# Putting all tiled matmuls of a chunk behind the first product's last rows, and eight banks as four and four

## The chip, the cores and the metric

The kernel runs on one core of a Trainium2 chip. The metric is the device time of one execution in microseconds (us). Engines are called by the profile's short names: PE (TensorE matmul), PEld (its weight load), DVE (VectorE), ACT (ScalarE), POOL (GpSimd) and SP (SyncE, which issues nearly all DMAs here, in order).

## The reference

An mLSTM cell over 4 batches x 8 heads x 768 steps of dimension 40, then a feed-forward layer with a squared ReLU over the 3072 resulting tokens:

```python
def _attn_ref(q, k, v, i_gate, f_gate, o_gate):
    for t in range(S):
        m_new = np.maximum(f_gate[:, :, t] + m, i_gate[:, :, t])
        f_stab = np.exp(f_gate[:, :, t] + m - m_new)
        i_stab = np.exp(i_gate[:, :, t] - m_new)
        m = m_new
        C = f_stab[..., None, None] * C + i_stab[..., None, None] * np.einsum('bhd,bhe->bhde', vt, kt)
        n = f_stab[:, :, None] * n + i_stab[:, :, None] * kt
        h_tilde = np.einsum('bhde,bhe->bhd', C, qt)
        nq = np.einsum('bhd,bhd->bh', n, qt)[:, :, None]
        y[:, :, t] = sigmoid(o_gate[:, :, t]) * h_tilde / np.maximum(np.abs(nq), 1.0)

def _moe_ref(x, w_in, w_out):          # x: 3072 x 320, w_in: 320 x 2048, w_out: 2048 x 320
    h = np.maximum(x @ w_in, 0.0)
    return h * h @ w_out
```

The weights w_in and w_out come as 64-bit floats.

## The kernel before

**Tiling.** The sequence is cut into 24 chunks of 128 steps (6 per batch). A chunk is worked in the parallel form: scores of keys against queries, times a matrix of decays W, give P; P times the values, plus the state C times the decayed queries, gives numerators and the denominator; the chunk's keys and weighted values, plus the decayed C, give the new C. Two chunks (256 tokens) make a token group of the feed-forward layer; there are 12 groups.

**Two stages.** The first stage (to about 100 us) handles chunks 0 to 5 with full-width matmuls while the 64-bit weights are rounded piece by piece (`Rounding`: `words` on ACT, `join` on DVE and POOL, one `step` is both). The second stage is one loop over `parts`, a list of triples (which product, group g, step i). Part n belongs to chunk s = 6 + n // 4 at place at = n % 4, so a chunk has four parts and a pair of chunks has eight: two steps of the second product of group g, four batches of the first product of group g+2, two more steps of the second product of group g. The steps of all engines are issued by hand in this loop's order (`manual_schedule`), and every engine and SP's queue work in that order.

**The first product** of a batch is `ffn1_main` (L634: full 128 x 128 tiles) and, for two batches together, `ffn1_rest` (L645: the last 64 of 320 rows, as two row tiles). ReLU on ACT (`relu_half`, L660) and squares on DVE (`square_half`, L667) follow. **The second product** is `ffn2` for group 0 (L674) and `ffn2_fast` after that (L728): seven products of half the width from sums of blocks, with DVE sums before (`sums`, L723) and after them (L744); the results leave by L764 and L769.

**A chunk of the second stage**, by functions: `load_squares` (L308) brings keys and queries in 32 x 32 squares and `turn_kq` (L315) turns them; `load_A` (L333), `decays` (L368), `mask` (L358), `weigh` (L382) make W; `scale_q` (L481) decays the queries; `scores` (L420, row tiles of 40 rows) and `weighted` (L433) make P. `attend_turned` puts the numerators (`numT`, L508 from C with 40 x 64 tiles, L517 from P with 128 x 64 tiles) into two PSUM banks, and the new C's product (`dC`, L527, 128 x 40 tiles) into a third; DVE turns numT (L534) and adds dC to the decayed C (L540; `decay_C`, L486).

**The relay.** A chunk's numerators then go to DRAM (`store_num`, L546) and back in another order (`load_num`, L551), `normalise_turned` (L563 to L572) divides, the rows go to DRAM (`store_rows`, L598) and back in squares (`load_rows`, L603), and `turn_squares` (L610) gives xT, which the first product of the chunk's token group reads. `pair_up` (L286) rearranges keys and queries of the chunk three later in DRAM. All these DMAs are in SP's queue, and each waits there for its data and for one of eight places.

**Places before.** At at = 0 `score` (scores and P); at at = 1, ahead of the part's product, `attend_turned`, then `decays`, `mask`, `turn_kq`, `decay_C`, `turn_squares` of the chunk before, `store_num`, `load`, `load_num`, `pair_up`; at at = 2 `scale_q`, and behind the product `weigh`, `normalise_turned`, `store_rows`, `load_squares`, `load_rows`, `load_A`; at at = 3 every fourth chunk the sigmoids. In a pair, the first chunk's tiled matmuls so stand between steps of the second product, and the second chunk's between batches of the first. The first product of group g+2 needs xT of the two chunks of the pair before.

**PSUM** has eight banks: attention 3 (`ps_at`), first stage's `ps_h` 3 and `ps_o` 2; in the second stage `ps_h` has 5.

Of the kernel before, what the change touches and what calls it, by code (L numbers as in the profile page):

```python
# [9 lines left out]
F32 = mybir.dt.float32  # L10
# [7 lines left out]
P = 128  # L18
# [11 lines left out]
def kernel(  # L30
# [48 lines left out]
    prep = ctx.enter_context(tc.tile_pool(name="prep", bufs=2))  # L79
    work = ctx.enter_context(tc.tile_pool(name="work", bufs=2))  # L80
    xts = ctx.enter_context(tc.tile_pool(name="xts", bufs=2))
    ps_at = ctx.enter_context(tc.tile_pool(name="ps_at", bufs=3, space=PSUM))
    banks = ExitStack()
    ps_h = banks.enter_context(tc.tile_pool(name="ps_h", bufs=3, space=PSUM))
    ps_o = banks.enter_context(tc.tile_pool(name="ps_o", bufs=2, space=PSUM))
    ctx.enter_context(tc.manual_schedule())
# [29 lines left out]
    def make_consts():  # L116
        for t in kq_b:
            nc.vector.memset(t[:, :, :, D:], 0.0)
        for t in va_b:
            nc.vector.memset(t[:, :, D:], 1.0)  # L120
        for t in va_w:
            nc.gpsimd.memset(t[:, H * D1 :], 0.0)
        nc.vector.memset(keep[:], 1.0)
        nc.vector.memset(keep[:, :, 0:1], 0.0)
        make_identity(nc, ident[:])

        nc.gpsimd.memset(sel[:], 0.0)
        nc.gpsimd.affine_select(
            sel[:], sel[:], compare_op=ALU.not_equal, fill=1.0, base=0, pattern=[[-1, H], [0, P]], channel_multiplier=1,
        )  # L130

        nc.gpsimd.memset(later[:], 0.0)
        nc.gpsimd.affine_select(
            later[:], later[:], compare_op=ALU.is_ge, fill=-1e30, base=0, pattern=[[1, P]], channel_multiplier=-1,
        )

        nc.gpsimd.memset(bdm[:], 1.0)
        nc.gpsimd.memset(bdm[:DP, :, 1, :], 0.0)
        nc.gpsimd.memset(bdm[DP:, :, 0, :], 0.0)


    def in_words(ap):
# [20 lines left out]
    class Rounding:  # L163
# [56 lines left out]
        def done(self):  # L220
            return len(self.b)

        def step(self):
            if len(self.b) < len(pieces):
                if len(self.a) == len(self.b):
                    self.words()
                self.words()
                self.join()

    rounding = Rounding()  # L230
# [94 lines left out]
    def sigmoid(s):  # L325
        nc.scalar.activation(st[s]["og"], st[s]["og"], AF.Sigmoid)
# [71 lines left out]
    def bank(o=False):  # L398
        t = ps_o.tile([P, W], F32, name="tp", tag="o_ps") if o else ps_at.tile([P, W], F32, name="tp", tag="at")
        return t[:].rearrange("p (j t) -> p j t", j=PR)  # L400

    def transposes(s, o=(False, False)):
        d = st[s]
        kqT(s)
        for i, n in enumerate(("kT", "qT")):
            tp = bank(o[i])
            for j in range(PR):
                nc.tensor.transpose(  # L408
                    tp[:, j, :], d["kq"][:, i, 2 * j : 2 * j + 2, :].rearrange("p h d -> p (h d)"), ident[:],
                )  # L410
            (nc.scalar.copy if i == 0 or s in (0, *range(2, 7)) else nc.vector.tensor_copy)(d[n], tp)
# [79 lines left out]
    def attend_turned(s):  # L491

        b, c = divmod(s, NB)
        d = st[s]
        halves = [slice(DP * i, DP * (i + 1)) for i in range(2)]
        live = [slice(DP * i, DP * i + D) for i in range(2)]  # L500
        numT = [ps_at.tile([P, W], F32, name="numT", tag="at")[:].rearrange("p (c t) -> p c t", t=P) for _ in range(2)]

        if c > 0:
            C = C_b[(s - 1) % 2]
            for e in range(2):
                for i, g in ((0, 0), (1, 1), (0, 1), (1, 0)):
                    j = 2 * e + g
                    nc.tensor.matmul(  # L508
                        numT[i][halves[g], e, :], lhsT=C[live[i], j * D1 : j * D1 + DP], rhs=d["eA"][live[i], j, :],
                        start=(e == 0), stop=False, skip_group_check=True,  # L510
                    )
        for i in range(2):
            for e in range(2):
                for g in range(2):
                    j = 2 * e + g
                    h = PR * i + j
                    nc.tensor.matmul(  # L517
                        numT[i][halves[g], e, :], lhsT=va_w[s % NKQ][:, h * D1 : h * D1 + DP],
                        rhs=d["P"][h % 2][:, h // 2, :] if s < KQ_SQ else d["P"][i][:, j, :],
                        start=(c == 0 and e == 0), stop=True, skip_group_check=True,  # L520
                    )
        if c + 1 < NB:
            dC = ps_at.tile([P, PR, D1], F32, name="dC", tag="at")
            for j in range(PR):
                for i in range(2):
                    h = PR * i + j
                    nc.tensor.matmul(  # L527
                        dC[live[i], j, :], lhsT=d["kq"][:, 0, h, :D], rhs=d["vw"][:, h, :], start=True, stop=True,
                    )

        tn = attn.tile([P, P // SQ, PR, SQ], F32, name="tn", bufs=1)
        to = tn[:].rearrange("p m c r -> p c m r")
        for i in range(2):
            nc.vector.transpose(to[:, 2 * i : 2 * i + 2], numT[i][:, :2, :].rearrange("p c t -> p (c t)"))  # L534
        d["tn"] = tn
        if c + 1 < NB:
            Cn = C_b[s % 2][:, : PR * D1].rearrange("p (j d) -> p j d", d=D1)
            for rows in live:
                if c > 0:
                    nc.vector.tensor_tensor(Cn[rows], dC[rows], d["Cd"][rows], op=ALU.add)  # L540
                else:
                    nc.vector.tensor_copy(Cn[rows], dC[rows])
# [229 lines left out]
    def do(f, s):  # L772
        if 0 <= s < NT:
            f(s)
# [36 lines left out]
    load_part(1, 2)  # L811
    fetch(1)
    idle(12)
    transposes(0)
    idle(4)
    scores(0)
    idle(3)
# [45 lines left out]
    for u in range(8):  # L863
        s = 2 + u // 2
        relu_half()
        if u % 2 == 0:
            if u == 0:
                ffn1(0, 0)
                scores(s)
                rounding.step()  # L870
            else:
                turn_rows(s - 1)
                scores(s)
                ffn1(u // 4, u % 4)
            if u == 2:
                rounding.words()
            weighted(s)
            if u == 2:
                mask(s + 1)
                rounding.join()  # L880
# [6 lines left out]
        else:  # L887
# [6 lines left out]
            attend(s)  # L894
            if u == 3:
                square_half()
            rounding.join()
            normalise(s)
            for r in {5: (8,), 7: (9,)}.get(u, ()):
                load(r)  # L900
            for r in {5: (7,), 7: (8,)}.get(u, ()):
# [18 lines left out]


    banks.close()
    ps_h = ctx.enter_context(tc.tile_pool(name="ps_h", bufs=5, space=PSUM))
    before.close()
    attn = ctx.enter_context(tc.tile_pool(name="attn", bufs=1))
    C_b = [attn.tile([P, PR * D1 + 24], F32, name=f"C{i}") for i in range(2)]
# [7 lines left out]
        parts += [(2, g, i) for i in range(2, 4)]  # L934
    LAST = (21, 23, 25, 25, 26)
    assert LAST[-1] == len(pieces)
    for n, (which, g, i) in enumerate(parts):
        s, at = 6 + n // 4, n % 4
        if n == 5:
            brought.close()  # L940
            late = ctx.enter_context(tc.tile_pool(name="late", bufs=1, side="right"))
        if at == 0:
            do(score, s)
        if at == 1:
            do(attend_turned, s)
            do(decays, s + 1)
            do(mask, s + 1)
            if n > 4:
                do(turn_kq, s + 1)
            do(decay_C, s + 1)  # L950
            if s > X_SQ:
                do(turn_squares, s - 1)
            do(store_num, s)
            do(load, s + 4)
            if 8 <= s < 20:
                load_o(s + 4)
            do(load_num, s)
            do(pair_up, s + 3)
        if 5 <= n < 8:
            sums_of_weights(n - 5)  # L960
        if n == 6:
# [7 lines left out]
            sums(g + 1, slice(0, NPAIR), (2,))  # L969
        if which == 2 and g > 1 and i < 2:  # L970
            sums(g, slice(0, NPAIR), (3 + i,))
        if at == 2:
            if n > 4:
                do(scale_q, s + 1)
        if at == 3:
            if s % 4 == 3:
                for r in range(s + 1, min(s + 5, NT)):
                    sigmoid(r)
        if which == 1:
            ffn1_main(g, i)  # L980
            if i % 2 == 0:
                held = st["half"]
            else:

                both = held, st["half"]
                for more, half in enumerate(both):
                    ffn1_rest(g, i - 1 + more, half[0])
                for half in both:
                    st["half"] = half
                    relu_half()  # L990
                    square_half()
        elif g == 0:
            ffn2(g, *divmod(i, 2))
        else:
            ffn2_fast(g, i)
        if at == 2:
            do(lambda s: weigh(s, masked=True), s + 1)
            if n < 4:
                do(turn_kq, s + 1)
                do(scale_q, s + 1)  # L1000
            do(normalise_turned, s)
            do(store_rows, s)
            do(load_squares, s + 2)
            do(load_rows, s)
            do(load_A, s + 2)
        if n < 5:
            while rounding.done < LAST[n]:
                rounding.step()


# [28 lines left out]
```

## Time and profile before

| | us |
|---|---|
| median of 3 runs (lowest, highest) | 527.99 (525.57, 529.61) |
| the profiled execution's own time | 527.05 |
| its span | 525.2 |
| L634 on PE, 768 matmuls | 175.7 |
| L728 on PE, 528 + 352 + 176 + 176 matmuls | 77.0 + 52.3 + 25.7 + 25.7 |
| tiled matmuls L645, L420, L517, L508, L527 on PE | 49.0, 26.9, 19.7, 10.4, 7.2 |
| DMA issue to landing, median: A_bc, num_rows, numerators back, x_rows, xT | 4.7, 3.1, 2.2, 2.1, 2.3 |

The profile is of one execution. Times are from the start of the span. A line of a timeline has the start, the time until the merged instructions' end, engine, line, operation, what is written and read, and how many instructions were merged; "idle" in brackets is the engine's idle time before them and what ended it. Matmuls overlap, so their cost in place is best read as the difference of starts. A line of the list of waits has who waited for whom, the total, how often, and the longest. A float32 matmul appears as two records.

### The profile page before, as it was taken

How to read it: one execution, taken by the hardware profiler on the slowest of the kernel's cores; microseconds unless marked ns; L12 is line 12 of the kernel's file. 1: busy time of each engine (PE TensorE's matmuls, PEld its weight loads, DVE VectorE, ACT ScalarE, POOL GpSimd, SP SyncE). 2: the span in 40 equal slices, each digit the busy share in tenths (PEclk: the TensorE clock that was granted, in tenths of full speed). 3: DMA queues.
4: the chain of work that ended last, by engine and by line, in shares of the span. 5: the costliest groups of instructions: out<-in, count | busy, mean ns of one | idle time of the engine just before them, and what ended most of it. 6: DMA issues, size and time to landing. Idle time of an engine off the chain costs nothing.

```text
span 525.2 us, 10338 instructions
## 1 busy us (share of the span) xinstructions
PE 515.1 (98%) x3929; PEld 449.8 (86%) x3929; DVE 331.8 (63%) x638; ACT 194.2 (37%) x460; POOL 88.2 (17%) x110
## 2 busy tenths in 40 slices
PE   9989989998999999999999999999999999999997
PEld 4868878885798898898898898898898898998997
DVE  8588988968864764655754755665755755522541
ACT  3767577552541431522432623322623413102000
POOL 3355633231210210110210200110201210000000
PEclk9997999999999999999999999999999999999999
DMA  9989699777586586586586576676556262110000
GB/s 193 225 207 194 158 161 202 190 184 155 117 162 121 126 173 126 124 168 127 135 162 132 122 151 125 149 158 135 133 122 128 69 130 43 61 36 2 26 25 26
DMA packets 239394, 68.06 MB, mean 130 GB/s; under 512 B 185744, under 2 KB 233872, under 8 KB 239344
## 3 DMA queue, kind: packets, MB, share of 16 engines
q1 hardware_dynamic: 239248, 67.20, 60.5%
q8 instruction: 31, 0.51, 0.4%
q10 hardware_dynamic: 96, 0.20, 0.1%
q14 instruction: 19, 0.16, 0.1%
HBM read 55.08 MB, written 17.86 MB: 139 GB/s over the span
## 4 chain that ended last, share of the span: by engine, by line
PE 87%; DVE 5%; ACT 3%; DMA 2%; SPq 2%; issue 1%; POOL 0%; ACTq 0%; DVEq 0%; POOLq 0%
PE h_ps L728 33%; PE h_ps L634 27%; PE h_ps L645 7%; PE tp L420 4%; PE numT L517 3%; PE h_ps L674 2%; PE hp L456 2%; PE numT L508 2%; PE idle L787 1%; DVE g L667 1%; PE tp L408 1%; SPq L308 1%; DMA num_rows<-tn 1%; PE A_ps L349 1%; PE dC L527 1%
## 5 line engine op out<-in xcount | busy, mean ns | idle before, releaser
L634 PE MATMUL h_ps<-xT,w_in 128*128 128x256 f32 x768 | 175.7, 384 | 0.6 <-ACT xT L619 0.6
L634 PEld LDWEIGHTS h_ps<-xT,w_in 128*128 128x128 f32 x768 | 144.2, 191 | 22.0 <-issue 1.2
L667 DVE TENSOR_TENSOR g<-r_sb 128x512 f32<-128x512 f32 x96 | 61.7, 702 | 66.5 <-ACT r_sb L660 66.5
L660 ACT ACTIVATE r_sb<-h_ps 128x512 f32<-128x512 f32 x96 | 49.9, 600 | 108.6 <-PE h_ps L645 105.5
L728 PE MATMUL h_ps<-w_out,g 128*128 128x160 f32 x528 | 77.0, 302 | 0.0
L728 PEld LDWEIGHTS h_ps<-w_out,g 128*128 128x128 f32 x528 | 72.5, 190 | 1.4
L358 POOL TENSOR_SCALAR_AFFINE_SELECT A_bc<-A_bc 128x1024 f32<-128x1024 f32 x22 | 24.3, 1103 | 214.2 <-ACT kq L368 155.4
L382 ACT ACTIVATE W_sb<-A_bc,b_T 128x128 f32<-128x128 f32 x176 | 53.8, 390 | 13.3 <-POOL A_bc L358 13.1
L728 PE MATMUL h_ps<-T,S 128*128 128x160 f32 x352 | 52.3, 302 | 0.0
L728 PEld LDWEIGHTS h_ps<-T,S 128*128 128x128 f32 x352 | 48.8, 190 | 3.0 <-ACT r_sb L660 3.0
L368 ACT ACTIVATE kq<-A_bc 64x512 f32<-64x512 f32 x30 | 18.9, 629 | 84.3 <-DMA A_bc<-a_rows 84.2
L645 PE MATMUL h_ps<-xT,w_in 64*128 64x256 f32 x384 | 49.0, 391 | 0.0
L645 PEld LDWEIGHTS h_ps<-xT,w_in 64*128 64x128 f32 x384 | 34.8, 186 | 12.3 <-issue 9.0
L744 DVE TENSOR_TENSOR y_sb<-y_sb,h_ps 128x160 f32<-128x160 f32 x44 | 14.1, 320 | 29.3 <-PE h_ps L728 28.7
L433 DVE TENSOR_TENSOR P_sb<-tp,W_sb 128x512 f32<-128x512 f32 x46 | 29.5, 684 | 3.6 <-PE tp L420 3.1
L534 DVE STREAM_TRANSPOSE tn<-numT 128x256 f32<-128x256 f32 x36 | 15.7, 447 | 23.2 <-PE numT L517 23.2
L394 POOL TENSOR_TENSOR vw<-va,W_sb 128x328 f32<-128x328 f32 x20 | 18.1, 904 | 66.0 <-ACT W_sb L382 60.3
L748 ACT COPY y_sb<-h_ps 128x160 f32<-128x160 f32 x11 | 3.2, 293 | 66.3 <-PE h_ps L728 66.3
L420 PEld LDWEIGHTS tp<-kqT 40*128 40x128 f32 x384 | 24.2, 187 | 3.3 <-issue 2.3
L420 PE MATMUL tp<-kqT 40*128 40x128 f32 x384 | 26.9, 279 | 0.0
L728 PE MATMUL h_ps<-T,g 128*128 128x160 f32 x176 | 25.7, 299 | 0.0
L728 PE MATMUL h_ps<-w_out,S 128*128 128x160 f32 x176 | 25.7, 299 | 0.0
(119 smaller groups left out, 592.0 us busy)
## 6 DMA issues: line engine op xcount, KB each, us to landing
A_bc<-a_rows SPq DMA_DIRECT2D x23, 512.0 KB, 4.7
raw<-in_moe_w_out_dram SPq DMA_DIRECT2D x16, 320.0 KB, 3.5
num_rows<-tn SPq DMA_DIRECT2D x18, 256.0 KB, 3.1
kq<-num_rows SPq DMA_DIRECT2D x72, 64.0 KB, 2.2
kqT<-kq_rows SPq DMA_DIRECT2D x34, 128.0 KB, 3.2
raw<-in_moe_w_in_dram SPq DMA_DIRECT2D x8, 512.0 KB, 5.2
kq<-in_k_dram SPq DMA_DIRECT2D x24, 160.0 KB, 4.7
va<-in_v_dram SPq DMA_DIRECT2D x24, 160.0 KB, 4.9
```

The lines of the kernel that those rows point to most:

```text
L358: nc.gpsimd.affine_select(A[:], A[:], compare_op=ALU.is_ge, fill=-1e30, base=0, pattern=[[0, H], [1, P]], channel_multiplier=-1,)
L368: nc.scalar.activation(e[rows], st[s]["A"][0][rows, PR * i : PR * (i + 1), :], AF.Exp)
L382: nc.scalar.activation(d["W"][:, i * n + h, :], A[i][:, h, :], AF.Exp, bias=b_T[:, b, c, i * n + h : i * n + h + 1],)
L394: nc.gpsimd.tensor_tensor(d["vw"][:], d["va"][:], d["W"][:, :, P - 1 : P].to_broadcast([P, H, D1]), op=ALU.mult,)
L420: nc.tensor.matmul(sc[i][:, j, :], lhsT=d["kT"][rows, j, :], rhs=d["qT"][rows, j, :], start=True, stop=True,)
L433: nc.vector.tensor_tensor(t, d["sc"][i], d["W"][:, heads, :], op=ALU.mult)
L517: nc.tensor.matmul(numT[i][halves[g], e, :], lhsT=va_w[s % NKQ][:, h * D1 : h * D1 + DP], rhs=d["P"][h % 2][:, h // 2, :] if s < KQ_SQ els ...
L634: nc.tensor.matmul(hs[i][:, n, :], lhsT=w_in[:, a, fb * P : (fb + 1) * P], rhs=xT[:, :, a, :], start=(n == 0 and a == 0), stop=False,)
L645: nc.tensor.matmul(hs[i][:, n, :], lhsT=w_in2[rows, 2 * pp + n, :], rhs=xT[rows, :, 2, :], start=False, stop=(n == 1),)
L660: nc.scalar.activation(rs[-1][:], h[:], AF.Relu)
L667: nc.vector.tensor_tensor(g4[:, :, i, :], r[:], r[:], op=ALU.mult)
L728: nc.tensor.matmul(to, lhsT=lhsT[:, p], rhs=rhs[:, p, :], start=(start and p == 0), stop=(p == NPAIR - 1), skip_group_check=True,)
```

## The change

Arithmetic and numbers of matmuls, of DMAs and of DVE work stay. The diff, cut to its core:

```diff
-    def transposes(s, o=(False, False)):
+    def transposes(s, o=(False, False), apart=0):
         for i, n in enumerate(("kT", "qT")):
+            if i > 0 and apart:
+                idle(apart)
...
         numT = [ps_at.tile(...) for _ in range(2)]
+        dC = numT[1][:, 2:, :]...                  
+        def new_kv():
...
+                        dC[live[i], j, :], lhsT=d["kq"][:, 0, h, :D], rhs=d["vw"][:, h, :],
+                        start=False, stop=True, skip_group_check=True,
...
         if c > 0:
...
+            if c + 1 < NB:
+                new_kv()
         for i in range(2):
...
-        if c + 1 < NB:
-            dC = ps_at.tile([P, PR, D1], F32, name="dC", tag="at")
...
+        if c == 0:
+            new_kv()
...
-    transposes(0)
+    transposes(0, apart=4)
...
             if u == 0:
                 ffn1(0, 0)
                 scores(s)
+                weighted(s)
+                relu_half()
                 rounding.step()
...
             if u == 3:
                 square_half()
-            rounding.join()
-            normalise(s)
+                normalise(s)
+                rounding.join()
+            else:
+                rounding.join()
+                normalise(s)
...
-    ps_h = ctx.enter_context(tc.tile_pool(name="ps_h", bufs=5, space=PSUM))
+    ps_at = ctx.enter_context(tc.tile_pool(name="ps_at", bufs=4, space=PSUM))
+    ps_h = ctx.enter_context(tc.tile_pool(name="ps_h", bufs=4, space=PSUM))
...
+    def attended(s):
+        do(store_num, s)
+        do(load, s + 4)
+        if 8 <= s < 20:
+            load_o(s + 4)
+        do(load_num, s)
+        do(pair_up, s + 3)
+    def normalised(s, *between):
+        do(normalise_turned, s)
+        do(store_rows, s)
+        for f, r in between:
+            do(f, r)
+        do(load_rows, s)
+    def ffn1_batch(g, i, squares=True, tiled=lambda: None):
+        both = st["held"], st["half"]
+        for more, half in enumerate(both):
+            ffn1_rest(g, i - 1 + more, half[0])
+        tiled()
+        for half in both:
+            st["half"] = half
+            relu_half()
+        if squares:
+            square_half()
+            square_half()
...
+        r, a = (n % 8, 6 + 2 * (n // 8)) if n >= 8 else (None, None)
+        if n in (0, 4, 8):
             do(score, s)
+            if n == 4:
+                square_half()
+                square_half()
+        if n in (2, 5):
+            attend_turned(s)
...
+        if r == 0:
+            do(load_squares, a + 2)
+            do(load_A, a + 2)
+        elif r == 1:
+            do(turn_squares, a - 1)
+            do(decays, a + 1)
+            do(mask, a + 1)
+            do(turn_kq, a + 1)
+        elif r == 4:
+            do(scale_q, a + 1)
+            do(turn_kq, a + 2)
+        elif r == 5:
+            normalised(a)
+        elif r == 7:
+            normalised(a + 1)
         if which == 1:
             ffn1_main(g, i)
...
+                    x = a + i // 2
+                    def tiled():
+                        do(attend_turned, x)
+                        do(score, x + 1)
+                    ffn1_batch(g, i, tiled=tiled)
+                    do(decay_C, x + 1)
+                    attended(x)
...
+        if r == 2:
+            do(lambda s: weigh(s, masked=True), a + 1)
+        elif r == 3:
+            do(decays, a + 2)
+            do(mask, a + 2)
+        elif r == 4:
+            do(lambda s: weigh(s, masked=True), a + 2)
+            do(load_A, a + 3)
+        elif r == 5:
+            do(load_squares, a + 3)
+        elif r == 6:
+            do(turn_squares, a)
+            do(scale_q, a + 2)
+        elif r == 7 and (a + 1) % 4 == 3:
+            for t in range(a + 2, min(a + 6, NT)):
+                sigmoid(t)
```

What it does, in words. From part 8 on, a pair of chunks a, a+1 is ordered by r = n % 8. In the parts r = 3 and r = 5, behind `ffn1_rest`, PE now has in a row: the last rows of the first product, `attend_turned` of a chunk, and the scores of the next. Chunk a stands behind the first two batches, chunk a+1 behind the second two. The new C's product moves into the unused half of the second numerator bank and, but for a batch's first chunk, ahead of L517. The attention has four banks and the feed-forward four; the attention's pool of the first stage ends with that stage.

On SP, the order of a pair becomes: kqT squares and A_bc of a+2; for a: numerators out, loads of a+4, numerators back, `pair_up`; A_bc of a+3; x_rows and xT of a; for a+1: numerators out, loads, numerators back, `pair_up`; kqT squares of a+3; an output; x_rows and xT of a+1; an output. On DVE, normalise of a stands at r = 5 ahead of that part's work, normalise of a+1 at r = 7, the turn of xT of a at r = 6 and of a+1 at r = 1 of the next pair.

In parts 0 to 7, `attend_turned` of chunk 6 moves from part 1 to part 2 and the squares of part 3 move behind P of chunk 7 in part 4; the rounding steps there no longer work one piece ahead at the end. In the first stage, four filler matmuls stand between the transposes of the first keys and queries, P of chunk 2 and a ReLU move ahead of a rounding step, and `normalise` of chunk 3 moves ahead of a `join`. Four memsets on POOL move to the end of the constants.

## The prediction

> **What bounds the kernel now.** I read the page first (busy shares, then the chain that ended last), then TensorE's list of waits, then the timeline of one steady stretch engine by engine, and last the windows around the two longest waits, for the granted clock.
>
> ```profile
> span 525.2 us, 10338 instructions
> PE 515.1 (98%) x3929; PEld 449.8 (86%) x3929; DVE 331.8 (63%) x638; ACT 194.2 (37%) x460; POOL 88.2 (17%) x110
> PE 87%; DVE 5%; ACT 3%; DMA 2%; SPq 2%; issue 1%; POOL 0%; ACTq 0%; DVEq 0%; POOLq 0%
> ```
>
> TensorE is busy for 98% of the span and holds 87% of the chain. Its waits are few, and all of them lie before 128 us:
>
> ```profile
> PE numT L508 <- DVE P_sb L433: 2.6, 1, 2.6
> PE tp L618 <- DVE x_sb L587: 1.7, 1, 1.7
> PE dC L449 <- DVE P_sb L433: 1.1, 1, 1.1
> ```
>
> From 155 to 465 us TensorE waits for nobody. One pair of chunks there takes 39.71 us (first product of one token group at 273.00, of the next at 312.71). TensorE's timeline of the same pair shows what a change of tile shape costs:
>
> ```profile
> 286.47 0.67 PE L508 MATMUL numT<-kq,C 40*64 40x128 f32 x16
> 288.40 3.72 PE L634 MATMUL h_ps<-xT,w_in 128*128 128x256 f32 x16
> 293.98 2.44 PE L728 MATMUL h_ps<-T,S 128*128 128x160 f32 x16
> 296.25 2.34 PE L728 MATMUL h_ps<-T,g 128*128 128x160 f32 x16
> 298.43 2.34 PE L728 MATMUL h_ps<-w_out,S 128*128 128x160 f32 x16
> 300.69 1.16 PE L420 MATMUL tp<-kqT 40*128 40x128 f32 x16
> ```
>
> Starts are to be subtracted: a product of L728 takes 2.18 us between like products (296.25 to 298.43) and about 2.27 beside a tiled one.
>
> The second thing to see is a relay off the critical path: what `attend_turned` computes goes to DRAM, back, through `normalise_turned`, to DRAM and back again before the first product (L634) of its token group may start. For chunk 17:
>
> ```profile
> 328.40 0.34 SPq L546 DMA_DIRECT2D num_rows<-tn  x1
> 331.45 1.85 SPq L551 DMA_DIRECT2D kq<-num_rows  x4
> 338.27 0.17 DVE L563 TENSOR_SCALAR dm<-kq 128x8 f32<-128x8 f32 x1
> 340.09 0.38 SPq L598 DMA_DIRECT2D x_rows<-x_sb  x1
> 343.35 2.16 SPq L603 DMA_DIRECT2D xT<-x_rows  x4
> 349.07 0.54 DVE L610 STREAM_TRANSPOSE xT<-xT 128x384 f32<-128x384 f32 x1
> 351.52 1.67 PE L634 MATMUL h_ps<-xT,w_in 128*128 128x256 f32 x7
> ```
>
> Its tiled matmuls began at 326.18, the user at 351.52: 25.3 us, with 1.9 to spare at the end.
>
> **The tile switches, pair by pair.** Nothing is computed less: the same matmuls run in another order. Before, one pair has five tiled groups on TensorE; after, two, each L645, L508, L527, L517, L420 in a row. Products: 6.71 + 4.54 + 4.45 = 15.70 before; all seven stand together after, 2.27 + 6 x 2.18 = 15.35. First product: 7.00 + 3.65 + 3.65 = 14.30 before, two runs of 7.00 after. Tiled matmuls: 9.7 before (1.83 + 1.93 for L645, 0.99 + 1.09 for L420, twice 0.60 + 0.92 + 0.41); after, between 4.85 and 5.05 a group, since L517 now meets another shape (1.02 as at 326.78) and L420 costs 0.99 or 1.09: 9.7 to 10.1. Sum 39.05 to 39.45, so 0.26 to 0.66 gained; I take 0.5, over eight pairs **-4.0 us**.
>
> **The banks.** The second product's pool goes from 5 banks to 4, the attention's from 3 to 4. With 4 each batch of the first product finds its banks freed by the ReLUs (2.06 us for four) about 2 us before it needs them, because the tiled group (2.95 us) stands between. The sum onto y (L744) that the third product of a half must wait for comes after transposes, new C, P and squares on VectorE (0.89 + 0.62 + 1.28 + 2.50 from the numerators' end at 1.9 us into the group), at 7.3 to 7.6 us, and that product may start at 7.4: 0.0 to 0.3 us a pair, hidden behind the wait told next.
>
> **The relay.** This is the term that decides. Let 0 be the start of a pair's first product. The second chunk's tiled group started at 13.5 us before; after, it stands behind both runs and both L645 groups: 7.00 + 1.93 + 2.95 + 7.00 + 1.90 = 20.8. The next pair's first product is due at 39.2, so the relay has 18.4 us instead of 25.3. Its steps, with the trace's durations and the new order of the queues:
> - numerators turned: L517 starts 1.0 us into the group (L508 and L527 first) and the second transpose ends 1.59 after that (326.78 to 328.37): 23.4.
> - The store of this chunk now stands in SP's queue behind the first chunk's x_rows and xT. That one's tn ends at 11.5; from there to numerators back in SBUF the trace shows 6.7 to 8.2 us where no A_bc load goes just ahead (odd chunks): 18.4; normalise 1.8: 20.3; x_rows 2.1 to land, four xT loads 2.1 to issue: **24.7**, 1.3 after tn is ready. A new A_bc load is issued shortly before that x_rows; numerator stores behind an A_bc (1.1 to 2.1 us) landed in 4.7 to 5.9 us instead of 2.0 to 3.4, so up to 2 us more.
> - 6.9 us to numerators back: 31.6. VectorE meets normalise after squares, sums and turns only at 32.0 (25.3 after P, squares to 27.8, then 0.3 + 1.2 + 0.3 + 0.5 + 0.7 + 1.2): ends 33.9.
> - SP behind the load of numerators: pair_up 2.45, four kqT loads 2.75 (moved ahead of x_rows), one output 0.4: free at 35.1, so x_rows leaves at 35.1 though ready at 33.9. Lands 37.3; xT issued by 39.3, landed 41.2, turned 41.8.
>
> So the first product starts at 42.0 instead of 39.2: 2.8 us late, 3.8 with the slow x_rows, 1.3 if both blockings of SP cost nothing but the VectorE order stays. I take 3.2. It hits token groups 4 to 11, which need chunks 9, 11 ... 23. Chunks 9 to 19 pay it in full. Chunk 21 has no loads of later chunks in SP's queue (VectorE's 32.0 binds, then 1.8 + 2.1 + 1.7 + 2.0 + 0.6 gives 40.4): 1.3. Chunk 23 has no scores, P or kqT work behind it: 0. **6 x 3.2 + 1.3 = +20.5 us.**
>
> The row speaks first on what these waits do to the clock: during the longest wait now, 2.6 us, the granted clock stayed at 1.00, while it fell to half around 39.4 us, after a stretch with a 1.1 us wait among small matmuls:
>
> ```profile
> 39.40:46.20 6.80, 6.71 (x35) 6.56 (x36) 5.48 (x11) 4.91 (x14) 4.16 (x6) 0.61 1.08 227
> 124.00:131.00 7.00, 4.40 (x56) 3.12 (x55) 6.41 (x14) 2.03 (x5) 0.86 (x1) 1.00 0.71 131
> ```
>
> (after the dash of times: PE, PEld, DVE, ACT, POOL busy, clock, DMA share, GB/s). By the row I charge nothing for the clock. The Trainium skill, "TensorE: Matmul & The Clock Gate", section "Why this matters for your kernels", warns of gaps above about 3 us between bursts, after which the clock is back at half; that rule speaks against this change, and if all six waits brought a half-clock stretch like the one above (6.8 us, 3.4 lost) the sum would be 20 us higher.
>
> **What else moves.** `decays`, `mask`, `weigh`, `scale_q`, `decay_C`, the turns of kqT and the sigmoids keep their number and are spread over other parts. ScalarE's eight exps (2.45) and GpSimd's mask (1.1), product (0.9) and decay (0.5) of a chunk now have 9 us or more from their input to their reader, and both engines are busy for under 40% of any pair: 0 as long as A_bc lands before the second part of a pair, which its issue 40 us earlier leaves open by far; 1.1 to 2.4 a chunk if it did not.
>
> **The start.** `normalise` ahead of `join` at the fourth half-step takes three VectorE passes (2.3 us) out of the way of L618: its wait of 1.7 goes, and the next input of that place, ScalarE's copy, is on time: -1.7. At the fourth part P of chunk 7 is put ahead of the four squares, but chunk 6's normalise stands before it and waits for a numerator load that starts 5.6 us later than now; I work out P at 126 against a need at 125, so of 2.6 some 1.3 goes (0 to 2.6). P of chunk 2 ahead of a rounding step frees L449 (1.1), but the sum over `hi` then stands behind that step and the squares (2.5 + 1.3), and the transposes of chunk 3 wait for its bank from 40.9 to about 42: 0, between -1.1 and +1. Four fillers between k's and q's transposes cost 4 x 0.22 less the 0.3 that q's arrival cost there and less slack before the scores: +0.4 (0 to 0.9). The moved memsets end long before their users: 0. Together **-2.6** (-5.4 to +1).
>
> **Sum.** 527.05 (the profiled execution's own time: the span of 525.2 and 1.8 around it) - 4.0 - 2.6 + 20.5 = 541.0. The median of the runs, 527.99, is 0.9 above that execution, less than the parts are sure to; I predict 541.
>
> **Rivals.** (1) The relay fits: x_rows and the numerator stores are served as soon as ready, and data land near the fast end (tn to numerators 6.7, x_rows 2.1): 23.4 + 6.7 + 1.8 + 2.1 + 1.7 + 2.0 + 0.6 = 38.3, under 39.2. Then only the gains stay: 528 - 6.6 = 521. For it: the orders are arranged for just this (normalise and xT's turn moved half a part earlier). Against: SP serves in order, and two of its blocks lie in the way. It decides up to a lateness of 0.2 us a pair. (2) Partly late, 0.2 to 1.3 us a pair, from shorter landings on a queue less crowded: 6 x 0.75 + 0 cancels the gains, 523 to 531. (3) As forecast, and half clock after some waits: three of them add 10, 551. (4) The change doesn't do what it says: each group still changes shape four times, and if those switches cost what the full ones did, the 4.0 are not there: 525 without a late relay, which I count within (2).
>
> **How the numbers follow.** Chances: forecast (1.3 to 3.8 late) 0.50, half clock on top (3) 0.12, (2) and (4) 0.20, (1) 0.18. One per cent of 528 is 5.3, about what a measurement tells here. Faster by over 1% (below 522.7) is (1) and a little of (2): 0.19. Within: the rest of (2) and the mildest forecasts: 0.18. Slower: 0.63. The range for 8 in 10 goes from 520, which still takes in most of (1), to 553, into (3). The forecast's own range is 529 (6 x 1.3 + 0) to 547 (6 x 3.8 + 2, fewer gains at the start).
>
> **What would show it.** Right: TensorE's list of waits has L634 (after: the first product) waiting for VectorE's turn of xT, six times or so, about 3 us each; in the chain DMA and SP gain some 5 to 10%; L420's wait for P and L618's are shorter; no group of L728 is split. Wrong: no such wait, with xT's turn ending before the last product of the pair; or SP's numerator store leaving right at tn's end; or a wait of L728 for L744 in each pair, which would say that VectorE, not the relay, binds.

## The result, and the profile after

The changed kernel takes 567.4 us (median of 4 runs, 560.16 to 570.03) beside 528.66 for the kernel before on the same chip (4 runs, 525.57 to 529.61): ratio 1.066, 95% interval 1.054 to 1.079. The ratio goes by the two faster runs alone (560.16 and 566.19), since the other two, the profiled one among them, lie over 1.5% above the fastest; the two medians stand at 1.073. It is slower, as forecast, but by nearly three times the forecast: 541 was predicted, 2.5% more than before, with a range up to 553.

The page of the profiled execution (570.03 us), with its span, the engines' busy time and the chain that ended last:

```profile
span 568.2 us, 10358 instructions
PE 531.1 (93%) x3932; PEld 461.0 (81%) x3933; DVE 328.6 (58%) x638; ACT 193.1 (34%) x460; POOL 90.8 (16%) x110
PE 60%; SPq 13%; DMA 12%; DVE 8%; issue 3%; ACT 2%; POOL 0%; DVEq 0%; POOLq 0%; ACTq 0%
```

TensorE's part of the chain fell from 87% to 60%; SP's queue, transfers and VectorE took it. TensorE's list of waits (what waited, for what; us in all, times, longest) names where:

```profile
PE h_ps L738 <- DVE y_sb L754: 21.9, 6, 4.5
PE h_ps L644 <- DVE xT L620: 7.4, 6, 2.7
```

The relay's wait (L644 for the turn of xT) is there six times, but with a quarter of the sum. Three quarters stand at a wait that the prediction had named only as what would prove it wrong: a product (L738) waits for a sum onto y (L754). One pair, chunks 14 and 15, shows how both come about. First SP's queue (start, us, instruction; these lines are issues):

```profile
319.75 3.18 SPq L561 DMA_DIRECT2D kq<-num_rows  x4
322.97 1.19 SPq L287 DMA_DIRECT2D kq_rows<-in_k_dram  x2
324.21 1.23 SPq L287 DMA_DIRECT2D kq_rows<-in_q_dram  x2
325.49 2.74 SPq L309 DMA_DIRECT2D kqT<-kq_rows  x4
328.33 0.51 SPq L774 DMA_DIRECT2D out_dram<-y_sb  x1
328.93 0.48 SPq L608 DMA_DIRECT2D x_rows<-x_sb  x1
331.52 1.86 SPq L613 DMA_DIRECT2D xT<-x_rows  x4
```

then VectorE's and TensorE's side of it (in brackets the idle time ahead and what ended it):

```profile
318.73 0.32 DVE L754 TENSOR_TENSOR y_sb<-y_sb,h_ps 128x160 f32<-128x160 f32 x1
326.12 0.20 DVE L582 COPY x_sb<-x_sb 128x64 f32<-128x64 f32 x1
331.02 0.32 DVE L754 TENSOR_TENSOR y_sb<-h_ps,y_sb 128x160 f32<-128x160 f32 x1 [3.34 <-DMA out_dram<-y_sb]
335.05 0.58 DVE L620 STREAM_TRANSPOSE xT<-xT 128x384 f32<-128x384 f32 x1 [2.58 <-DMA xT<-x_rows]
```

```profile
324.56 2.34 PE L738 MATMUL h_ps<-w_out,g 128*128 128x160 f32 x16
331.39 4.63 PE L738 MATMUL h_ps<-w_out,g 128*128 128x160 f32 x16 [4.50 <-DVE y_sb L754]
335.82 1.54 PE L644 MATMUL h_ps<-xT,w_in 128*128 128x256 f32 x5
```

One token group's y1 (the first of its two output tiles) is ready at 319.05. Its store (L774) is issued at 328.33, since SP must first load the numerators, copy k and q for later chunks (L287) and load their transposes (L309). The sum u12 of the next group (L754) reuses that very buffer, one of three, and can run only at 331.02; the next product writes the PSUM bank that this sum reads, and so starts behind it. Meanwhile x_rows (L608), in the same queue behind the same loads, was ready at 326.32 and left at 328.93; xT is turned at 335.63, and the next first product starts 0.19 later. So two chains end within 5 us of each other, and waiting for the first hides most of the wait for the second.

From the trace, for the second chunk of each pair: the time from the pair's first product to the numerators turned (tn), from there to xT turned, and from first product to next first product.

```
chunk             9     11     13     15     17     19     21     23
before: tn      15.66  15.66  15.66  15.66  15.66  15.66  15.66  15.66
  tn to turn    22.14  21.24  22.14  22.14  21.24  22.14  22.14  17.86
  pair          39.71  38.81  39.71  39.71  38.81  39.71  39.71  35.99
after: tn       25.27  23.27  22.98  23.58  23.46  24.91  24.26  24.89
  tn to turn    22.74  22.42  20.83  22.57  20.89  21.94  18.16  15.29
  pair          48.06  45.75  43.87  46.34  44.40  46.91  42.48  40.23
```

Before, 1.9 us were left at the end of every pair but the last (2.5). After, the next first product stands 0.05 to 0.19 us behind the turn in all eight: the relay closes every loop, though the wait list puts most of the idle time on L738. A pair with nothing late would take 7.10 + 1.93 + 3.03 twice and 15.32 for seven products (so long wherever none of them waits), 39.44 (0.61 less where a chunk has no C yet, as in the pairs of 13 and 19; 0.34 less where none is made, 11 and 17; 1.4 less for the last). Over that the eight pairs lost 8.6 + 6.7 + 5.0 + 6.9 + 5.3 + 8.1 + 3.0 + 2.2 = 45.8 us. The two profiled executions are 43.0 apart: the first of these pairs also begins 3.0 us earlier than before, at 151.79 instead of 154.77.

The rows of tn show a third thing. After the change tn is 23.0 to 23.6 for chunks 11 to 17, but 24.3 to 25.3 for 9, 19, 21 and 23. There a stretch at half clock, which came with the wait just before, reaches into the first product. The first and the second run of it in the last pair show the cost:

```profile
469.61 8.79 PE L644 MATMUL h_ps<-xT,w_in 128*128 128x256 f32 x32 [2.21 <-DVE xT L620]
483.28 7.17 PE L644 MATMUL h_ps<-xT,w_in 128*128 128x256 f32 x32
```

The granted clock is 0.50 from 469.50 to 472.91. Against pairs with the same tiled matmuls at full clock, tn is late by 1.7, 1.9, 0.7 and 1.6 us for these four chunks: some 6 of the 45.8 us, an estimate from the table.

### The profile page after: what moved, and what is told of

It is laid out like the page before. It is cut to its first block, busy times and chain, and to the rows that moved or that the text cites. A ratio compares the mean times of both kernels' runs of the same rounds, so it can differ in the third digit from the quotient of the medians.

```text
span 568.2 us, 10358 instructions
## 1 busy us (share of the span) xinstructions
PE 531.1 (93%) x3932; PEld 461.0 (81%) x3933; DVE 328.6 (58%) x638; ACT 193.1 (34%) x460; POOL 90.8 (16%) x110
## 4 chain that ended last, share of the span: by engine, by line
PE 60%; SPq 13%; DMA 12%; DVE 8%; issue 3%; ACT 2%; POOL 0%; DVEq 0%; POOLq 0%; ACTq 0%
PE h_ps L644 27%; PE h_ps L738 11%; PE h_ps L655 7%; PE tp L423 3%; DMA xT<-x_rows 3%; DMA x_rows<-x_sb 3%; SPq L561 3%; SPq L309 3%; PE numT L533 2%; DMA kq<-num_rows 2%; SPq L613 2%; SPq L287 2%; PE hp L459 2%; PE idle L797 1%; DVE g L677 1%
## 5 line engine op out<-in xcount | busy, mean ns | idle before, releaser
L644 PE MATMUL h_ps<-xT,w_in 128*128 128x256 f32 x768 | 180.0, 393 | 8.1 <-DVE xT L620 7.4
L644 PEld LDWEIGHTS h_ps<-xT,w_in 128*128 128x128 f32 x768 | 148.7, 197 | 33.3 <-DVE xT L620 9.8
L738 PE MATMUL h_ps<-w_out,g 128*128 128x160 f32 x528 | 87.6, 326 | 21.9 <-DVE y_sb L754 21.9
L738 PEld LDWEIGHTS h_ps<-w_out,g 128*128 128x128 f32 x528 | 82.9, 211 | 23.4 <-DVE y_sb L754 23.3
L677 DVE TENSOR_TENSOR g<-r_sb 128x512 f32<-128x512 f32 x96 | 64.4, 729 | 20.4 <-ACT r_sb L670 20.4
L738 PE MATMUL h_ps<-T,S 128*128 128x160 f32 x352 | 52.3, 302 | 0.0
L738 PEld LDWEIGHTS h_ps<-T,S 128*128 128x128 f32 x352 | 48.7, 190 | 1.4 <-ACT r_sb L670 0.3
L359 POOL TENSOR_SCALAR_AFFINE_SELECT A_bc<-A_bc 128x1024 f32<-128x1024 f32 x22 | 27.4, 1243 | 111.0 <-ACT kq L369 93.5
L489 POOL TENSOR_TENSOR Cd<-C,kq 128x164 f32<-128x164 f32 x15 | 7.0, 464 | 158.8 <-DVE C L550 131.3
L620 DVE STREAM_TRANSPOSE xT<-xT 128x384 f32<-128x384 f32 x18 | 10.3, 575 | 27.2 <-DMA xT<-x_rows 27.1
L738 PE MATMUL h_ps<-T,g 128*128 128x160 f32 x176 | 25.7, 299 | 0.0
L738 PE MATMUL h_ps<-w_out,S 128*128 128x160 f32 x176 | 25.7, 299 | 0.0
```

What stands on the lines that cost most here:

```text
L359: nc.gpsimd.affine_select(A[:], A[:], compare_op=ALU.is_ge, fill=-1e30, base=0, pattern=[[0, H], [1, P]], channel_multiplier=-1,)
L644: nc.tensor.matmul(hs[i][:, n, :], lhsT=w_in[:, a, fb * P : (fb + 1) * P], rhs=xT[:, :, a, :], start=(n == 0 and a == 0), stop=False,)
L677: nc.vector.tensor_tensor(g4[:, :, i, :], r[:], r[:], op=ALU.mult)
L738: nc.tensor.matmul(to, lhsT=lhsT[:, p], rhs=rhs[:, p, :], start=(start and p == 0), stop=(p == NPAIR - 1), skip_group_check=True,)
```

## The experiments

All times below stand beside the kernel before, run on the same chip (527.97 to 529.4). Three questions: is it the y store, the relay, or both; does the half clock that follows such waits cost anything; and is it the order of SP's queue, or the transfers themselves?

**Another order in SP's queue.**

```diff
 r==5: -normalised(a)              +normalise_turned(a); store_rows(a)
 attended(a+1): store_num  +load_rows(a)  load  load_num  pair_up
 r==5 end: -load_squares(a+3)      r==7: normalised(a+1)  +load_squares(a+3)
 turn_kq(a+1): r==1 -> r==2
```

> The changed kernel with three y buffers as it is, and SP's queue in another order: the second chunk's numerator store goes ahead of the first chunk's xT loads, and the kqT loads of chunk a+3 go from ahead of y1's store and x_rows to behind the second chunk's xT loads (their turn on VectorE half a part later). Theory A (queue blocking by SP's order makes both chains late, by about 6.8 us beyond the last product in the pair at 331): numerator stores leave within 0.5 us of tn, x_rows within 1.3 of its data, y1's store before L754 needs the buffer; TensorE's waits fall from 29 us to under 6 and the half-clock stretches with them; time 520 to 530. Rival C (the transfers themselves are slow in this crowd, whatever their order): waits of 15 us or more stay; time 545 to 565.

558.5 us (ratio 1.055, 1.048 to 1.062). L738's waits fell from 21.9 to 3.5 and L644's grew from 7.4 to 20.7. The numerator store left 0.03 us after tn instead of 3.1 to 4.4, but the load of numerators then stood 2.3 to 4.5 behind its data, after xT loads and the loads of k, v and the gate. Theory A's mechanism held, its number failed: one block went, another came. Rival C's time and waits came too, so this run alone does not part the two.

**The product's wait filled with work.** Eighteen matmuls of zeros ahead of the product that waits, in six pairs.

```diff
         elif step == 1:
+            if 1 < g < 8:
+                warm(18)
             product(Y, g4[:, :, 0, cols[1]], B12)
```

> The changed kernel with 18 matmuls of zeros (about 0.22 us each, 4.0 us) put ahead of the product that waits for L754 in the six pairs where it waits, so that TensorE works through its waits; they write a bank of their own and nothing reads it. Theory A says of the 40 us that about 20 are half clock after the waits and the rest the waits themselves: the stretches at half clock in the second stage fall from nine (41 us) to three or fewer, the pair's waits stay as long in all (filled instead of idle), time 545 to 557. Rival D (the half clock costs nothing that the late chains would not cost anyway, since TensorE waits for the same releases): clock back near 1.00 but time 562 to 570, with the waits longer by what the clock gave.

569.82 us (1.076, 1.070 to 1.083), no faster than the changed kernel. Two lines of TensorE's timeline of this run:

```profile
325.81 4.10 PE L806 MATMUL warm<-zeros 128*128 128x512 bf16 x17
329.75 2.33 PE L738 MATMUL h_ps<-w_out,g 128*128 128x160 f32 x16
```

The product that took 4.63 us at half clock takes 2.33 here, and the granted clock is 1.00 from 246 us to the end; in the changed kernel eight stretches between 152 and 473 us, 41 us in all (the expectation had counted nine), are at half. Yet the pairs are nearly as long (45.7 on the mean of chunks 9 to 19, against 45.9): L644 waits for the relay instead (13.1 us). Rival D held in the main. What the profile does show shorter is tn, 23.0 to 23.6 in all pairs but chunk 13's, the only one that a half-clock stretch reached (24.7); with it the eight pairs are 354.0 us instead of 358.1. The medians show no gain.

**Buffers for y, nothing else.** Two more buffers for both halves of y would be the plainest test, but they do not fit: the pool `old` needs 5.125 KB a partition, and 3.09 would be left. So the tile of the sum u12 gets two buffers of its own instead.

```diff
-st["y"] = [ffn.tile(..., name="y_sb", bufs=3) for _ in range(2)]
+st["y"] = [ffn.tile(..., name="y_sb", bufs=3), late.tile(..., name="y0_sb", bufs=2)]
```

> The changed kernel with two buffers of their own for the sum u12 and three for the other half of y, nothing else, so that L754 needs no store of the group just before. Theory A (the relay of the second chunk would end nearly as late as the y store, about 335.7 against 335.8 in the pair at 331): L738's waits for L754 (21.9 us) go, L644's waits for xT grow from 7.4 to 22 to 30, time 560 to 568. Theory B (the y store alone binds): L644's waits stay under 8 and time falls to 525 to 545.

581.71 us (1.097, 1.094 to 1.101): slower still. The waits of this run:

```profile
PE h_ps L644 <- DVE xT L620: 25.6, 6, 5.7
PE h_ps L644 <- DMA kqT<-kq_rows: 10.2, 2, 5.5
PE h_ps L738 <- DVE y_sb L754: 8.5, 6, 3.0
```

Theory B fell, and theory A's time (560 to 568) was missed by far. Without the y store the relay alone holds TensorE, for more than both chains did. The two waits put down to kqT are the relay's as well: in the first of them xT is turned at 295.68 and the product starts at 295.73. So is L738's wait, in that pair at least: the sum stands behind `normalise_turned` on VectorE, which sat idle for 2.77 us until the numerators were back. Here the half-clock stretches all lie behind the relay's waits, in the first product: tn is 25.0 to 26.1 in seven of the eight pairs, some 15 us in sum. (The relay was longer too, 21.7 to 24.9 us from tn to turn for chunks 9 to 19; why, these runs do not settle.)

**The relay cut off, and both cut off.** A constant tile takes xT's place in the first product (in `ffn1_rest` too, not shown) from the fourth token group on, so that the output is not the reference's; the relay still runs. The second kernel has the buffers for y as well.

```diff
-rhs=xT[:, :, a, :],
+rhs=xT[:, :, a, :] if g < 3 else st["flat"][:],
```

> The changed kernel, but from the fourth token group on the first product reads a constant tile instead of xT: that part of its result is left out, and TensorE no longer waits for the relay, which still runs with all its transfers and VectorE work. Theory A (two chains, each late by itself): L738's waits for L754, that is for y1's store behind the relay's and later chunks' loads in SP's queue, stay at 12 us or more, time 540 to 560. Theory G (the relay is the only chain; the y store was late only because the relay's lateness kept it so): under 5 us of waits, time 517 to 527.

> The same constant tile, and two buffers of their own for u12 and three for the other half of y: neither chain holds TensorE. This shows what the change would bring if both chains were in time. From the terms: 528 less 0.36 a pair in eight pairs and 2 to 4 at the start, so 520 to 524 with no wait over 0.5 us in the second stage. If a third chain is late too (P, kqT or the banks), its waits show by name and the time is over 527.

With the relay cut alone: 562.65 us (1.063, 1.058 to 1.068), and this wait (its lines stand two further down: L740 is the product, L756 the sum):

```profile
PE h_ps L740 <- DVE y_sb L756: 26.5, 6, 5.1
```

So the y store, behind the relay's transfers in SP's queue, is a chain of its own, nearly as costly by itself as the change; theory G fell. With both cut: 544.46 us (1.029, 1.022 to 1.035), not the 520 to 524 expected. Of 17.7 us of waits that were left in the second stage, 16.1 name the sums onto y again (L756, 10.4 at L644's banks and 5.7 at L740). VectorE's timeline has the reason:

```profile
281.94 0.58 DVE L620 STREAM_TRANSPOSE xT<-xT 128x384 f32<-128x384 f32 x1 [5.14 <-DMA xT<-x_rows]
282.44 1.20 DVE L316 STREAM_TRANSPOSE kqT<-kqT 128x1024 f32<-128x1024 f32 x1
283.57 0.28 DVE L756 TENSOR_TENSOR y_sb<-y_sb,h_ps 128x160 f32<-128x160 f32 x1
```

VectorE works in order: while it waits for xT (5.14 us here), the sum behind the turn waits too, and with it the bank that TensorE needs. The late relay has a third way to TensorE.

**Numerators' load ahead of later chunks' loads** (on top of the first order):

```diff
 attended: store_num, load_rows(a), +load_num, load, load_o, -load_num, pair_up
```

> The order of the first order run, and the numerators' load ahead of the loads of k, v and the gate of later chunks, instead of behind them. In the first order run the second chunk's numerators went out at once, but their load stood 2.3 to 4.5 us after they had landed, behind xT loads, k, v and the gate. Theory A (the relay's place in SP's order is the whole loss): that delay falls under 0.5, tn to numerators back from 10 to 6.5 to 7.5 us, L644's waits from 20.7 to under 3 us in sum, the pair at 39.2 to 39.8 us, time 519 to 526. Rival C (crowded transfers land later as more is sent at once): numerators back stays at 9 us or more, time over 540.

556.19 us (1.051, 1.047 to 1.054): a miss. Numerators still took 7.8 to 9.6 us to come back (the store landed in 3.3 to 4.9, and xT loads held the load up by as much as 1.6), and x_rows, which had left at once in the first order, now left 1.6 to 3.2 us late behind k, v and pair_up.

**The second chunk's relay on ScalarE's queue**, SP's order untouched, and the same with the buffers for y.

```diff
+def own(s): return nc.scalar if s > 8 and s % 2 else nc.sync
-nc.sync.dma_start(...)   +own(s).dma_start(...)   (store_num, load_num, store_rows, load_rows)
```

> The changed kernel with SP's order untouched, and the second (odd) chunk's four transfers of the relay (numerator store, their load, x_rows, xT; chunks 9 to 23) issued from ScalarE's queue, where nothing of SP stands ahead. In the last order run the numerators still took 7.8 to 9.6 us to come back and x_rows left 1.6 to 3.2 us late, behind loads in SP's queue, and 14 us of waits for xT were left. Theory A (SP's serving in order is the loss, wherever it is): store within 0.1 of tn, back in 6 to 7 us, x_rows at once, so the relay ends about 5 to 7 us earlier than in the changed kernel, and y1's store, no longer behind the odd chunk's load, leaves earlier too; TensorE's waits from 29 to under 8 us, time 520 to 532. Rival C (the crowd of transfers, not the queue, delays them): landings of numerators and x_rows stay over 3 us, waits over 15, time over 540. Rival E (ScalarE blocked by the four transfers delays its copies of y and the ReLUs): TensorE waits for L758, L763 or the first product's banks instead, time 535 to 560.

> The same with two buffers of their own for u12 and three for the other half of y. Theory A: if y1's store is in time in the run before, the same within 1%; if L738 waits for L754 or L758 there, these waits go and the time falls by at most their sum. With the changed kernel's own queue the buffers alone made it slower (581.7), because SP's kqT loads then met L644; if that comes again here, this one is slower than the run before.

577.92 us (1.095, 1.091 to 1.098) and 577.13 us (1.095, 1.090 to 1.099). Rival E's mechanism held, at a higher price than it named: in the first, L741 (the product) waits 38.6 us for ScalarE's copy of y (L761). In the second of the two, ScalarE's timeline:

```profile
323.64 0.39 ACTq L611 DMA_DIRECT2D x_rows<-x_sb  x1
326.26 2.13 ACTq L616 DMA_DIRECT2D xT<-x_rows  x4
328.42 1.28 ACT L327 ACT_TABLE_LOAD   x1 [16.00 <-DMA xT<-x_rows]
329.71 1.55 ACT L327 ACTIVATE og<-og 128x320 f32<-128x320 f32 x4
331.17 0.27 ACT L761 COPY y_sb<-h_ps 128x160 f32<-128x160 f32 x1
```

The xT loads wait for x_rows, and the copy that TensorE needs waits behind them. The store left 0.03 us after tn; the block had only moved to another queue.

**The whole relay first.** SP's order by who is waited for; VectorE's normalise ahead of the turn. TensorE's order is the change's.

```diff
 attended(s): store_num, load_num, load_rows(first chunk), load, load_o   (pair_up out)
 r==2 end: turn_kq(a+1), weigh, +pair_up(a+3), +pair_up(a+4), +load_A(a+3)   (from r==3, 5 and 4)
 r==6 end: +normalised(a+1) (from r==7), +load_squares(a+3), turn_squares(a)
```

> The changed kernel with the relay of both chunks ahead of everything else in SP's queue: numerator store and load at once, xT loads of the first chunk behind them, loads of k, v and gate next; pair_up and A_bc of later chunks moved to the third part of a pair, where SP has nothing of the relay, kqT loads of a+3 behind the second chunk's xT; on VectorE the second chunk's normalise ahead of the turn of the first chunk's xT and of the next half's sum. Nothing in TensorE's order is changed. Theory A (SP's serving in order, and then VectorE's, make the relay late): numerators back 5 to 6.5 us after tn, x_rows 7 to 9 us after tn, xT turned 14 to 16 us after tn of the odd chunk instead of 19 to 21; TensorE waits under 5 us in sum and a pair takes 39.2 to 39.8; time 517 to 526, faster than both kernels. Rival C (the relay's four trips through DRAM are too long for 18.4 us whatever the order): waits over 15 us, time over 535.

540.89 us (1.023, 1.020 to 1.027). From tn to turn the relay now takes 16.4 to 17.6 us for chunks 9 to 19, under the 18.4 that it has, with the same transfers. So their order made the relay late, not their own length: rival C falls. The relay's waits are gone (L644 for xT: 0.4 us); in their place L738 waits 10.9 us in seven pairs for VectorE's sum S2 (L733), which now stands behind the turn of the first chunk's xT:

```profile
304.64 0.20 DVE L582 COPY x_sb<-x_sb 128x64 f32<-128x64 f32 x1
306.02 0.58 DVE L620 STREAM_TRANSPOSE xT<-xT 128x384 f32<-128x384 f32 x1 [1.18 <-DMA xT<-x_rows]
306.52 0.65 DVE L484 TENSOR_TENSOR kq<-kq,kqT 128x512 f32<-128x512 f32 x1
307.09 1.21 DVE L733 TENSOR_TENSOR S<-S,g 128x1024 f32<-128x1024 f32 x1
```

**That turn moved behind S2**, and the same with the first half-step's old order.

```diff
-r==6 end: turn_squares(a)      +r==7, behind sums(g+1, (2,)): turn_squares(a)
```

> The last kernel with one instruction of VectorE moved back: the turn of the first chunk's xT goes behind the sum S2 (L733), which the third of the last four products waits for. In the last run the relay was in time (0.4 us of waits for xT in all), but the turn, put ahead of S2, waited for its xT loads, and the product waited for S2: 10.9 us in seven pairs. Theory A: that wait goes, a pair takes 39.2 to 39.6 us, the change's gains appear: the profiled span 10.9 less than 536.9, and 1 to 3 more by the half clock after those waits; time 525 to 530, the same as before or just faster. Rival F (another step of the relay or a y store is just as late as S2 was): waits of over 6 us by another name, time 533 to 541.

> The same, with the orders of the very first half-step as they were before the change (P of chunk 2 behind the rounding step). The change's order there removed a wait of 1.1 us for P (L449) and brought one of 1.9 for num (L411). Theory A: 0.5 to 1 us faster than the run before it, or the same if P's place is what keeps the wait of the following transposes short; 524 to 530.

534.74 us (1.011, 1.008 to 1.014) and 535.33 (1.013, 1.010 to 1.015). Most of the loss is back, by orders of SP and VectorE alone: the ratio fell from 1.066 to 1.011. From tn to turn the relay now takes 16.5 to 18.4 us for chunks 9 to 19, pairs 40.1 to 41.4, and these waits are left:

```profile
PE h_ps L644 <- DVE xT L620: 4.4, 5, 1.6
PE h_ps L738 <- DVE S L733: 3.1, 3, 1.6
PE h_ps L738 <- DVE y_sb L754: 1.4, 1, 1.4
```

TensorE is idle for 18.2 us of this span and for 10.1 of before's. Relay, S2 and y now compete for VectorE within the same few microseconds; no order tried serves all three. The first half-step's order makes no difference beyond the intervals.

**The start alone.** The kernel before with only the orders of the first stage changed.

```diff
+transposes(0, apart=4)
 u==0: scores(s), +weighted(s), +relu_half(), rounding.step()
 u==3: square_half(), +normalise(s), rounding.join()   (-normalise behind join)
```

> The kernel before with only the orders of the first stage changed as the change has them (fillers between k's and q's transposes, P of chunk 2 ahead of a rounding step, normalise ahead of join at the fourth half-step). The trace of the changed kernel has the first matmul of the second stage 1.2 us earlier, and its third product 3.8 us earlier, of which the second stage's own reorder (P ahead of the squares) makes the rest. Expected here: 0.5 to 2 us less than before (526.0 to 527.5), L618's wait gone, a new wait for num in the transposes. A rival: the wait at the transposes of chunk 3 (1.9 us) with the fillers costs what the rest brings: same or up to 1 slower.

527.13 us beside 529.40 (0.9952, 0.9927 to 0.9977): 2.3 us, half a per cent, faster, a little beyond the expected 0.5 to 2. L618's wait fell from 1.7 to 0.2, a wait of 1.9 for num came where L449 had waited 1.1. It is the only version here that is faster than both kernels.

## Why the prediction was wrong in size

- **Direction and kind: right.** The relay decides, the tiled group later in the pair is why, and "SP serves in order" is the reason: orders of SP and VectorE alone brought the ratio from 1.066 to 1.011. Chain shares for DMA and SP rose by 10 and 11 points; 5 to 10 had been said.
- **Tiled group and tn: right at full clock.** tn was put at 23.4; 23.0 to 23.6 were measured in four pairs, and 24.3 to 25.3 where half clock reached into the first product.
- **The relay's length: the step that failed.** "So the first product starts at 42.0 instead of 39.2" took 18.4 us from tn to turn. It was 20.8 to 22.7 for chunks 9 to 19. Mis-sized were its two blocks in SP: the numerator store "1.3 after tn is ready" left 3.1 to 4.4 after it, since x_rows of the first chunk landed in 3.7 to 5.4 us, and the xT loads ahead waited for that; and x_rows, "at 35.1 though ready at 33.9", left 1.3 to 3.4 late. The pairs lost 5.0 to 8.6 us instead of 3.2, chunk 21's 3.0 instead of 1.3 (whose own sum, 32.0 + 1.8 + 2.1 + 1.7 + 2.0 + 0.6, is 40.2 and not 40.4), the last 2.2 instead of 0. The slow x_rows had been seen ("up to 2 us more") but only half counted. Chunk 7's xT also came 2.7 us late, which was not in the sum at all.
- **The y store: missed.** "One output 0.4" was priced as an instruction of SP, but not who waits for it. Under "the banks" the sum L744 was timed by VectorE's order alone (0.0 to 0.3 us); it also needs a y buffer, whose store stands behind 8.5 us of loads in SP's queue. Before, no product waited for it; after, it is a chain that costs nearly as much alone (562.65 with the relay cut).
- **Tile switches: right kind, 0.27 a pair** (39.71 to 39.44), at the low end of the 0.26 to 0.66, against 0.5 taken: 2.2 us, not 4.0. A run of the first product took 7.10, not 7.00.
- **The start: right in sign, its parts less so.** Of the -2.6, 1.3 belong to P of chunk 7, which the run of the start does not contain: that run shows -2.3 where -1.3 was the sum. In the changed kernel the wait for P of chunk 7 is gone whole (2.6, not 1.3), but TensorE then waits as long for chunk 7's xT (2.7).
- **The clock: charged nothing, and that was short.** Waits of 2.2 to 4.5 us each brought 3.4 or 6.8 us at half clock, while the 2.6 us wait before had brought none. The Trainium skill ("TensorE: Matmul & The Clock Gate", "Why this matters for your kernels") names gaps above about 3 us. Four of the eight waits here were longer than that, four shorter (2.2 to 2.8). Where the half clock fell on the product behind the y store's wait, it ran in time that the relay left anyway, and filling those waits did not lower the median. Where it reached into the first product, it made tn, and with it the relay, late: some 6 us here, and some 15 in the run with buffers for y. So rival (3) came true in kind beside the late relay.
- **Rivals.** "The relay fits" is ruled out for the change as it is; the last reordered kernels come close to it and still lose 1%. The condition named for a wrong prediction, L738 waiting for the sum, did come, though not because VectorE binds: in the pair shown it idled 3.34 us for the store.

## What to carry to other kernels

When a step is moved later in a loop, give each chain that hangs on it its full length with the queue's new neighbours, and for every transfer that the move pushes back ask who waits for its buffer, not what its issue costs. The longest wait in a list need not be the bound: cut each chain alone and both together before mending one, since here each by itself kept nearly the whole loss. Order an in-order queue by who is waited for first; moving the waiting transfers to another engine's queue only moved what they blocked. Half clock after a wait was free here where another late chain covered it, and was paid where it ran on into the loop's first product.

## What was not expected of the hardware

The clock fell to half after waits of 2.2 us, not only of 4.5, and stretches came in lengths of 3.41 or 6.83 us; whether a wait near 2.6 us brought one differed: 2.51 us did in the changed kernel, 2.60 in the kernel before and 2.92 with the relay cut off did not. The store x_rows issued just behind a 512 KB load of A_bc landed in 3.7 to 5.4 us (chunks 8 to 18) instead of 2.1, and that delay reached the four xT loads behind it and, through them, the next chunk's numerator store.
